# Sharing two of a quad's 32 score tiles between ScalarE and VectorE in the second full-attention layer

## The chip, the core and the metric

The kernel runs on one core of a Trainium2 chip. Its engines are TensorE (PE, with its weight loads as PEld), VectorE (DVE), ScalarE (ACT), GpSimd (POOL) and SyncE (SP), which here issues the DMAs. The metric is the device time of one execution in microseconds (us); lower is better. A difference under 0.2% is not told from no change.

## The reference

Four attention layers follow each other on x of 2048 positions by 512 features; layers 0 and 2 use weights A and a window of 256 keys, layers 1 and 3 use weights B and all keys. Everything is float32, with 32 heads of 16 features.

```python
def _B_ref(x, wqkv, wo):                     # _A_ref: the same, with a causal window of 256
    B, S, D = x.shape                        # 1, 2048, 512
    H = 32; Dh = D // H
    qkv = (x @ wqkv).reshape(B, S, 3, H, Dh).transpose(2, 0, 3, 1, 4)
    q, k, v = qkv[0], qkv[1], qkv[2]
    scores = jnp.einsum("bhqd,bhkd->bhqk", q, k) * Dh ** -0.5
    p = softmax(scores, axis=-1)
    o = jnp.einsum("bhqk,bhkd->bhqd", p, v)
    return o.transpose(0, 2, 1, 3).reshape(B, S, D) @ wo

x = A_x
x = x + _A_ref(_layernorm(x), A_wqkv, A_wo)
x = x + _B_ref(_layernorm(x), B_wqkv, B_wo)
x = x + _A_ref(_layernorm(x), A_wqkv, A_wo)
x = x + _B_ref(_layernorm(x), B_wqkv, B_wo)
```

## The kernel before, in words

The layers are numbered 0 to 3 (`l`); layer 3 is the second full one. In a full layer the work is cut into quads: `c` is one of 4 blocks of 512 queries, `qd` one of 8 groups of 4 heads. Layer 3 goes through them as `t` (two groups of heads) outside, `c` next and the two `qd` inside, 32 quads in all.

Within a quad, `attn_full` runs over 16 tiles `j` of 128 keys, and in each over two pairs of heads `pr`. `exps` writes the transposed scores of one tile and one pair, 128 keys by 2 heads by 512 queries, into a score buffer `s` of two PSUM banks, one bank for each head (L764, eight matmuls of 32 keys each). There are two such buffers. ScalarE then takes both banks in one instruction, exp(scale x s), into a tile `e` of SBUF (L772). There is no maximum to subtract here: a bound on the scores is added inside the matmul by extra rows of the keys and queries. The matmuls with the values follow about two tiles later, when `flush` runs the closure `pv` (L817): eight for a tile, four heads by two halves of the keys, each head into its own 32 partitions of the accumulators `acc`. A column of ones in the values `V` gives the softmax's denominator, and `epilogue` divides at the end of a quad, so a factor common to all of a quad's exponentials drops out.

Between the tiles stands side work: projections of queries, keys and values for later quads and the output projection of earlier ones. `Side.step` and `Side.share` deal it out in small pieces by a modelled clock, a budget and a `lag` that holds pieces back while PE is charged with more than its share. Its results collect in one PSUM buffer `b`, and VectorE joins the two halves into SBUF (L428, L429 by `join`, or L714 for the output). VectorE's short operations wait in queues `VQ`, which `drain` hands out one at a time by the same clock, the queue with the lowest number first.

In layer 3 the orders of PE and of VectorE are those in which the code is written out; the other engines' orders are made by a scheduler. The tag `xh` has four buffers of 2 KB per partition; the layer norms of earlier layers used them.

Of the kernel before, what the change touches and what calls it, by code (L numbers as in the profile page):

```python
# [9 lines left out]
F32 = mybir.dt.float32  # L10
# [3 lines left out]
I32 = mybir.dt.int32  # L14
AF = mybir.ActivationFunctionType
ALU = mybir.AluOpType
# [3 lines left out]
P = 128  # L20
NT = S // P
# [3 lines left out]
QC = 512  # L25
# [165 lines left out]
def fast_path(ctx, tc, flag, a_x, a_wqkv, a_wo, b_wqkv, b_wo, out):  # L191
# [20 lines left out]
    XC, XN, V, O, OT, KM, PH = {}, {}, {}, {}, {}, {}, {"free": 0.0, "busy": False}  # L212
# [13 lines left out]
    def vec(us):  # L226

        vt_[0] = max(vt_[0], clock[0]) + us
# [59 lines left out]
    nc.gpsimd.memset(onesf, 1.0)  # L288
    nc.gpsimd.memset(ones, 1.0)
    nc.gpsimd.memset(zeros, 0.0)  # L290

    nc.gpsimd.memset(hsum, 1.0)
    nc.gpsimd.affine_select(hsum, hsum, pattern=[[-DH, 32]], compare_op=ALU.is_ge,
# [458 lines left out]
        if u:  # L752
            soon(1, 1.2, parts)

    def exps(name, kt, qt, pr, pieces):

        ps = ps_s.tile([P, 2, QC], F32, name=f"s{name}", tag="s")
        w0 = min(p[3] for p in pieces)
        w1 = max(p[3] + p[2] for p in pieces)
        for kc, qc, wd_, s0 in pieces:  # L760
            if PH["full"]:
                for g in range(0, P, 32):
                    for h in range(2):
                        nc.tensor.matmul(ps[g:g + 32, h], kt[R * h:R * h + R, pr, kc + g:kc + g + 32],  # L764
                                         qt[R * h:R * h + R, pr], start=True, stop=True, skip_group_check=True)
                continue
            for h in range(2):
                nc.tensor.matmul(ps[:, h, s0:s0 + wd_], kt[R * h:R * h + R, pr, kc:kc + P],  # L768
                                 qt[R * h:R * h + R, pr, qc:qc + wd_], start=True, stop=True)
        spent(0.27)  # L770
        e = pp.tile([P, 2, QC], F32, name=f"e{name}", tag="e", bufs=EB)
        nc.scalar.activation(e[:, :, w0:w1], ps[:, :, w0:w1], AF.Exp, scale=SCALE)  # L772
        return e

    def flush(n):
# [27 lines left out]
        return kt, qt  # L803

    def attn_full(l, c, qd, kt, qt, a):
        for j in range(NT):
            es_ = []
            for pr in range(2):
                es_.append(exps(f"{l}_{c}_{qd}_{j}_{pr}", kt[j // 8], qt, pr, [(j % 8 * P, 0, QC, 0)]))
                if pr == 0:  # L810
                    yield None

            def pv(j=j, es_=es_):
                for h in range(4):
                    for r in range(2):
                        k = slice(R * r, R * r + R)
                        nc.tensor.matmul(acc[r][32 * h:32 * h + DH + 1, :], V[l, qd // 4, j // 8][k, j % 8, 4 * (qd % 4) + h, :],  # L817
                                         es_[h // 2][k, h % 2, :], start=(j == 0), stop=(j == NT - 1),
                                         skip_group_check=True)
            yield pv  # L820


# [202 lines left out]
    def attention(l, works):  # L1025

        win = l % 2 == 0
        phase(l)
        load = load_win if win else load_full
        sd = None  # L1030
        for t in range(NHT if l == 3 else 1):
            for c in range(NQ):
                qds = range(2 * t, 2 * t + 2) if l == 3 else range(NQD)
                if l == 1:

                    sd = sd or Side(NT * NQD // 2, works[0], works[1], 0.33)
                    while ("Q", 1, c) not in DONE or pend and PH["busy"]:
                        sd.one(True)
                    settle()
                else:  # L1040
                    sd = Side((3 if win else NT) * len(qds), works[t * NQ + c], works[t * NQ + c + 1], 0.34 if l == 3 and t < 2 else 0.0)
                ahead = deque([PRE.pop("w", None) or load(l, c, qds[0])])
                if win:
                    ahead.append(load(l, c, 1))
                for qd in qds:
                    if (l, c, qd) == (1, 0, NQD // 2):
                        sd.finish()
                        sd = Side(NT * NQD * NQ - NT * NQD // 2, works[1], works[2], 0.33)
                    while (l, c, qd % 2) == (1, 0, 1) and qd + 1 in qds and ("S", 1, (qd + 1) // 2) not in DONE:
                        if ("K1", (qd + 1) // 2) in DONE and not PH["busy"]:  # L1050
                            settle()
                        else:
                            sd.one(True)
                    ops = ahead.popleft()
                    if qd + 1 + win in qds:
                        ahead.append(load(l, c, qd + 1 + win))
                    a = acc[qd % 2 if win else 0]
                    began, u = clock[0], 0
                    for f in (attn_win if win else attn_full)(l, c, qd, *ops, a):
                        drain()  # L1060
                        if f is None:
                            flush(1)
                            if u == 1:
                                sd.step()
                            continue
                        clock[0] = max(clock[0], began + (2.4 if win else 1.8))
                        began = clock[0]
                        pvq.append([f])
                        if win:
                            flush(2)  # L1070
                            sd.step()
                            settle(False)
                        elif u == 0:
                            flush(1)
                        elif u:
                            sd.step()
                        while not win and (c, qd, u) == (0, 0, NT - 5) and ("V", l, 3, (0,), 2) not in DONE:
                            sd.one(True)
                        drain()
                        u += 1  # L1080
                    pvq[-1].append(lambda l=l, c=c, qd=qd, a=a: epilogue(l, c, qd, a))
                if l != 1 or c == NQ - 1:
                    sd.finish(l == 3 and (t, c) != (NHT - 1, NQ - 1))
                if not win and not PH["busy"]:
                    settle()
        flush(0)
        drain(4)
        phase(None)
# [208 lines left out]
```

## Time and profile before

| | us |
|---|---|
| median of 3 runs | 2695.24 (2694.04 to 2697.39) |
| profiled execution | 2692.26 |
| its span, from the first to the last instruction | 2690.2 |
| first exponential of layer 3 starts | 1709.2 |
| last exponential of layer 3 starts | 2669.2 |

The prediction quotes rows of the profile. In a row of a group, the line and engine come first, then the operation, what it writes and reads, partitions by elements, and the count; after the bar the busy time in us and the mean length of one in ns; after the second bar the engine's idle time just before these instructions and which instructions ended it. In a timeline row the first two numbers are start and length in us, and instructions of one kind are merged. Successive instructions of one engine overlap a little, so lengths add up to more than the time that they take together. The TensorE clock granted is 0.991 of full speed over the span.

### The profile page before, as it was taken

How to read it: one execution, taken by the hardware profiler on the slowest of the kernel's cores; microseconds unless marked ns; L12 is line 12 of the kernel's file. 1: busy time of each engine (PE TensorE's matmuls, PEld its weight loads, DVE VectorE, ACT ScalarE, POOL GpSimd, SP SyncE). 2: the span in 40 equal slices, each digit the busy share in tenths (PEclk: the TensorE clock that was granted, in tenths of full speed). 3: DMA queues.
4: the chain of work that ended last, by engine and by line, in shares of the span. 5: the costliest groups of instructions: out<-in, count | busy, mean ns of one | idle time of the engine just before them, and what ended most of it. 6: DMA issues, size and time to landing. Idle time of an engine off the chain costs nothing.

```text
span 2690.2 us, 120844 instructions
## 1 busy us (share of the span) xinstructions
PE 2474.9 (92%) x54767; PEld 1133.5 (42%) x54767; DVE 1107.5 (41%) x2350; ACT 2363.6 (88%) x2671; POOL 531.8 (20%) x1072
## 2 busy tenths in 40 slices
PE   7889999999998999999999999899999999999997
PEld 3344444444443444444444444544444443433332
DVE  5576453223334434434236666232333323333333
ACT  4666764999999999999996776699999999999997
POOL 1556550000000100100116886010000000000000
PEclk9999999999999999999999999999999999999999
DMA  8889875232334325324227666433333323334332
GB/s 281 254 274 268 236 198 155 69 97 86 110 94 120 97 91 148 103 87 115 92 77 211 189 171 166 128 95 105 98 97 97 106 77 114 106 98 126 126 118 93
DMA packets 341189, 361.29 MB, mean 134 GB/s; under 512 B 117800, under 2 KB 256568, under 8 KB 334392
## 3 DMA queue, kind: packets, MB, share of 16 engines
q1 hardware_dynamic: 340664, 353.46, 44.2%
q8 instruction: 430, 7.05, 1.1%
q14 instruction: 95, 0.78, 0.1%
HBM read 240.65 MB, written 96.99 MB: 126 GB/s over the span
## 4 chain that ended last, share of the span: by engine, by line
ACT 55%; PE 23%; issue 11%; DVE 6%; DMA 3%; SPq 1%; POOL 0%; ACTq 0%; DVEq 0%; POOLq 0%
ACT e L772 55%; PE b L406 7%; PE acc L850 4%; PE acc L817 3%; PE s L764 2%; PE s L768 2%; PE bs L409 2%; PE b L409 2%; PE b L402 1%; DMA kt<-kw 1%; DVE xh L461 1%; DVE xn L455 0%; DMA qs<-sp 0%; SPq L483 0%; DVE xh L455 0%
## 5 line engine op out<-in xcount | busy, mean ns | idle before, releaser
L772 ACT ACTIVATE e<-s 128x1024 f32<-128x1024 f32 (+2 forms) x2432 | 2241.6, 1056 | 143.2 <-PE s L768 104.5
L817 PE MATMUL acc<-e,vt 64*17 64x512 f32 x16384 | 1094.6, 590 | 1.9 <-issue 1.9
L764 PE MATMUL s<-qt,kt 64*32 64x512 f16 x16384 | 860.0, 381 | 123.9 <-ACT e L772 97.1
L764 PEld LDWEIGHTS <-kt 64*32 64x32 f16 x16384 | 408.2, 89 | 935.1 <-issue 853.8
L817 PEld LDWEIGHTS acc<-e,vt 64*17 64x17 f32 x16384 | 283.8, 92 | 67.9 <-issue 8.1
L843 POOL TENSOR_SCALAR_AFFINE_SELECT e<-e 128x256 f32<-128x256 f32 x512 | 230.5, 457 | 154.8 <-ACT e L772 154.1
L840 POOL TENSOR_SCALAR_AFFINE_SELECT e<-e 128x256 f32<-128x256 f32 x448 | 201.5, 456 | 96.5 <-ACT e L772 93.2
L850 PE MATMUL acc<-e,vt 128*17 128x384 f32 (+2 forms) x2816 | 202.6, 390 | 2.5 <-POOL e L840 2.2
L749 POOL TENSOR_TENSOR oh<-o,oh 128x512 f16<-128x512 f32 x31 | 36.1, 1165 | 725.1 <-DVE oh L748 725.1
L428 DVE TENSOR_SCALAR sa<-acc 128x512 f32<-128x512 f32 x64 | 44.3, 691 | 291.3 <-PE acc L817 291.3
L406 PE MATMUL b<-xc,w 128*32 128x512 f16 x2496 | 152.4, 389 | 10.8 <-DVE km L575 6.9
L714 DVE SCALAR_TENSOR_TENSOR x<-b,x 128x512 f32<-128x512 f32 x122 | 84.0, 689 | 175.1 <-PE b L402 168.4
L534 POOL TENSOR_TENSOR sq_h<-sp_h 128x512 bf16<-128x512 f16 x29 | 43.0, 1483 | 562.4 <-DVE sp_h L528 562.4
L768 PE MATMUL s<-qt,kt 64*128 64x384 f16 (+2 forms) x1408 | 120.8, 276 | 28.2 <-ACT e L772 22.7
L534 POOL TENSOR_TENSOR sq<-sp 128x512 bf16<-128x512 f16 x32 | 45.8, 1434 | 496.8 <-DVE sp L528 473.6
L402 PE MATMUL b<-xc,w 64*32 64x512 f16 x3072 | 126.4, 376 | 1.5 <-DVE j L429 0.8
L428 DVE TENSOR_SCALAR vt<-b 128x256 f32<-128x256 f32 (+1 forms) x36 | 18.4, 512 | 233.8 <-PE b L402 219.9
L402 PE MATMUL b<-wo,oh 64*32 64x512 f16 x2592 | 109.1, 376 | 4.1 <-DVE m_None L591 1.8
L402 PE MATMUL b<-xc,w_h 64*32 64x512 f16 x2784 | 111.8, 376 | 0.1
L428 DVE TENSOR_SCALAR j_h<-b 128x512 f32<-128x512 f32 x29 | 20.1, 692 | 214.6 <-PE b L402 214.6
L406 PEld LDWEIGHTS <-w 128*32 128x32 f16 x2496 | 73.5, 99 | 79.2 <-issue 27.7
L768 PEld LDWEIGHTS <-kt 64*128 64x128 f16 x1408 | 52.2, 94 | 125.7 <-issue 105.3
(142 smaller groups left out, 1942.3 us busy)
## 6 DMA issues: line engine op xcount, KB each, us to landing
kt<-kf SPq DMA_DIRECT2D x128, 512.0 KB
qt<-qs SPq DMA_DIRECT2D x128, 256.0 KB
xd<-x SPq DMA_DIRECT2D x96, 256.0 KB
x<-xd SPq DMA_DIRECT2D x96, 256.0 KB
w<-wd SPq DMA_DIRECT2D x21, 1024.0 KB
kt<-kw SPq DMA_DIRECT2D x64, 256.0 KB
qs<-sp SPq DMA_DIRECT2D x48, 256.0 KB
wo<-wd SPq DMA_DIRECT2D x12, 1024.0 KB
```

The costliest lines, as they stand in the source:

```text
L402: nc.tensor.matmul(ps[g:g + 32, r], a[k, g:g + 32], b[k], start=(i == 0), stop=(i == len(pairs) - 1), skip_group_check=True)
L406: nc.tensor.matmul(ps[g:g + 32], a[:, g:g + 32], b, start=(i == 0), stop=(i == len(pairs) - 1), skip_group_check=True)
L409: nc.tensor.matmul(ps, a, b, start=(i == 0), stop=(i == len(pairs) - 1))
L534: nc.gpsimd.tensor_tensor(sq, sp[:, 0], sp[:, 0], ALU.mult)
L714: nc.vector.scalar_tensor_tensor(xs[i], p, 1 / WS, xs[i], op0=ALU.mult, op1=ALU.add)
L764: nc.tensor.matmul(ps[g:g + 32, h], kt[R * h:R * h + R, pr, kc + g:kc + g + 32], qt[R * h:R * h + R, pr], start=True, stop=True, skip_grou ...
L768: nc.tensor.matmul(ps[:, h, s0:s0 + wd_], kt[R * h:R * h + R, pr, kc:kc + P], qt[R * h:R * h + R, pr, qc:qc + wd_], start=True, stop=True)
L772: nc.scalar.activation(e[:, :, w0:w1], ps[:, :, w0:w1], AF.Exp, scale=SCALE)
L817: nc.tensor.matmul(acc[r][32 * h:32 * h + DH + 1, :], V[l, qd // 4, j // 8][k, j % 8, 4 * (qd % 4) + h, :], es_[h // 2][k, h % 2, :], star ...
L840: nc.gpsimd.affine_select(v, v, pattern=[[0, 2], [-1, P]], compare_op=ALU.is_gt, fill=0.0, base=0, channel_multiplier=1)
L843: nc.gpsimd.affine_select(v, v, pattern=[[0, 2], [1, P]], compare_op=ALU.is_ge, fill=0.0, base=0, channel_multiplier=-1)
L850: nc.tensor.matmul(a[32 * h:32 * h + DH + 1, q * P:(q + nb) * P], V[l, (4 * c + j) // 4][:, j % 4, 4 * qd + h, :], es_[h // 2][:, h % 2, s ...
```

## The change: VectorE makes one head of two tiles

In layer 3, the second pair of heads (`pr` = 1) of key tiles `j` = 4 and `j` = 9 is shared. ScalarE takes one bank of 512 columns; VectorE reads the other (`OWN` says which) and makes its exponential in eight instructions. The first scales the score to a base-2 exponent in fixed point, bounds it from below and writes it as int32. Two bit operations split that into a power of two `e` and a fraction `u`, and five steps of a polynomial give `p`. The first is issued at once; the other seven go into a new queue `VQ[4]`, behind the four that there were. The tiles `u`, `e` and `p` use the tag `xh`. The polynomial's form gives twice the exponential, so each of ScalarE's exponentials of this layer gets the bias ln 2, from a tile of 128 by 1 that POOL fills at the start. The matmuls of `pv` leave the two heads out, and `late` issues them together behind tile 14 of the quad; it first hands out what is left of `VQ[4]`.

```diff
+OWN = {4: 1, 9: 0}
+POLY = (-0.2122642642036666, 20.582234973412888, 57.43304580516819, 188.4105936388931, 265.3878017523131)
+OWN_AT = 12
+LEAD, LOW = 0x40000000 | 0x761904, -117.0
...
-    VQ, vt_ = [deque() for _ in range(4)], [0.0]
+    VQ, vt_ = [deque() for _ in range(5)], [0.0]
...
+    ln2 = cp.tile([P, 1], F32, name="ln2")
+    nc.gpsimd.memset(ln2, 0.6931471805599453)
...
+    def own_exp(name, s, got):
+
+        u, e, p = (vp.tile([P, QC], F32, name=f"{n}{name}", tag="xh", bufs=XNB) for n in ("ou", "oe_", "op_"))
+        ui, ei = u.bitcast(I32), e.bitcast(I32)
+        with tc.high_priority(HEAD_START):
+            nc.vector.tensor_scalar(ui, s, SCALE * 1.4426950408889634 * 2.0 ** 23, LOW * 2.0 ** 23, op0=ALU.mult, op1=ALU.max)
+        vec(0.75)
+        ops = [(0.45, lambda: nc.vector.tensor_scalar(ei, ui, 0x7F800000, LEAD, op0=ALU.bitwise_and, op1=ALU.bitwise_xor)),
+               (0.45, lambda: nc.vector.tensor_scalar(ui, ui, 0x7FFFFF, 0x3E800000, op0=ALU.bitwise_and, op1=ALU.bitwise_or))]
+        for i, k in enumerate(POLY):
+            ops.append((0.7, lambda i=i, k=k: nc.vector.scalar_tensor_tensor(p, p if i else u, k / 4.0 ** (i + 1), e if i == 4 else u,
+                                                                            op0=ALU.add, op1=ALU.mult)))
+        got["left"] = got.get("left", 0) + len(ops)
...
+        for us, f in ops:
+            VQ[4].append((clock[0] + 0.6, us, lambda f=f: one(f)))
+        return p
...
-        nc.scalar.activation(e[:, :, w0:w1], ps[:, :, w0:w1], AF.Exp, scale=SCALE)
+        if own is not None:
+            nc.scalar.activation(e[:, 1 - own], ps[:, 1 - own], AF.Exp, bias=ln2, scale=SCALE)
+            got[name] = own_exp(name, ps[:, own], got)
+        elif got is not None:
+            nc.scalar.activation(e, ps, AF.Exp, bias=ln2, scale=SCALE)
+        else:
+            nc.scalar.activation(e[:, :, w0:w1], ps[:, :, w0:w1], AF.Exp, scale=SCALE)
...
+                own = OWN.get(j) if l == 3 and pr else None
+                es_.append(exps(f"{l}_{c}_{qd}_{j}_{pr}", kt[j // 8], qt, pr, [(j % 8 * P, 0, QC, 0)], own, got))
...
+                mine = OWN if l == 3 else {}
+                for h in range(4):
+                    if j not in mine or h != 2 + mine[j]:
+                        head(j, h, es_[h // 2][:, h % 2], j == NT - 1)
+
+                def late():
+                    while got["left"]:
+                        vec(VQ[4][0][1])
+                        VQ[4].popleft()[2]()
+                    for i, own in mine.items():
+                        head(i, 2 + own, got[f"{l}_{c}_{qd}_{i}_1"], False)
+                    spent(0.86)
+                if j == OWN_AT and mine:
+                    PH["late"] = late
...
                         elif u:
+                            if PH["late"]:
+                                PH["late"]()
+                                PH["late"] = None
+                                sd.lag += 0.86
                             sd.step()
```

The rows below show the program's order of instructions on an engine. Names are those of the code with block, quad, tile and pair: `e_2_3_4_1` belongs to block 2, quad 3, tile 4, pair 1 (all rows are of layer 3). ScalarE around that tile, before:

```order
L772 ACTIVATE e_2_3_3_1_46688<-s_2_3_3_1_46679 128x1024
L772 ACTIVATE e_2_3_4_0_46699<-s_2_3_4_0_46690 128x1024
L772 ACTIVATE e_2_3_4_1_46718<-s_2_3_4_1_46709 128x1024
L772 ACTIVATE e_2_3_5_0_46768<-s_2_3_5_0_46759 128x1024
```

and after:

```order
L803 ACTIVATE e_2_3_3_1_46949<-s_2_3_3_1_46940,ln_88 128x1024
L803 ACTIVATE e_2_3_4_0_46960<-s_2_3_4_0_46951,ln_88 128x1024
L800 ACTIVATE e_2_3_4_1_46979<-s_2_3_4_1_46970,ln_88 128x512
L803 ACTIVATE e_2_3_5_0_47025<-s_2_3_5_0_47016,ln_88 128x1024
```

The tile of pair 1 is half as long, and every row reads the bias tile besides its scores.

VectorE around the same tile, before (`j` and `vt` are joins of a query projection and of a value projection, `m` and `km` belong to the bound on the scores):

```order
L428 TENSOR_SCALAR j_1_2_h_2_46657<-b_37140 128x512
L429 SCALAR_TENSOR_TENSOR j_1_2_h_2_46657<-b_37140,j_1_2_h_2_46657 128x512
L528 CAST sp_1_2_h_2_46720<-j_1_2_h_2_46657 128x512
L529 TENSOR_TENSOR sp_1_2_h_2_46720<-j_1_2_h_2_46657,sp_1_2_h_2_46720 128x512
L428 TENSOR_SCALAR vt_1_1_43761<-b_37140 128x16x16
L429 SCALAR_TENSOR_TENSOR vt_1_1_43761<-b_37140,vt_1_1_43761 128x16x16
```

and after, with the read of the score bank at L766:

```order
L434 TENSOR_SCALAR j_1_2_h_2_46918<-b_37142 128x512
L435 SCALAR_TENSOR_TENSOR j_1_2_h_2_46918<-b_37142,j_1_2_h_2_46918 128x512
L766 TENSOR_SCALAR ou_2_3_4_1_46981<-s_2_3_4_1_46970 128x512
L534 CAST sp_1_2_h_2_47009<-j_1_2_h_2_46918 128x512
L535 TENSOR_TENSOR sp_1_2_h_2_47009<-j_1_2_h_2_46918,sp_1_2_h_2_47009 128x512
L768 TENSOR_SCALAR oe_2_3_4_1_46982<-ou_2_3_4_1_46981 128x512
L769 TENSOR_SCALAR ou_2_3_4_1_46981<-ou_2_3_4_1_46981 128x512
L771 SCALAR_TENSOR_TENSOR op_2_3_4_1_46983<-ou_2_3_4_1_46981 128x512
L771 SCALAR_TENSOR_TENSOR op_2_3_4_1_46983<-op_2_3_4_1_46983,ou_2_3_4_1_46981 128x512 x2
L434 TENSOR_SCALAR vt_1_1_43958<-b_37142 128x16x16
L435 SCALAR_TENSOR_TENSOR vt_1_1_43958<-b_37142,vt_1_1_43958 128x16x16
L771 SCALAR_TENSOR_TENSOR op_2_3_4_1_46983<-op_2_3_4_1_46983,ou_2_3_4_1_46981 128x512
```

The read stands behind a join here, and the polynomial's steps stand between the joins that the side work needs.

PE at the end of the same quad, before, goes from the last scores of tile 14 to the first of tile 15:

```order
L764 LDWEIGHTS kt_2_3_1_45812
L764 MATMUL s_2_3_14_1_47221<-qt_2_3_45808,kt_2_3_1_45812 32x512
L764 LDWEIGHTS kt_2_3_1_45812
L764 MATMUL s_2_3_15_0_47232<-qt_2_3_45808,kt_2_3_1_45812 32x512
L764 LDWEIGHTS kt_2_3_1_45812
```

and after:

```order
L791 LDWEIGHTS kt_2_3_1_46051
L791 MATMUL s_2_3_14_1_47490<-qt_2_3_46047,kt_2_3_1_46051 32x512
L853 MATMUL acc_81<-op_2_3_4_1_46983,vt_0_0_36722 17x512
L853 MATMUL acc_82<-op_2_3_4_1_46983,vt_0_0_36722 17x512
L853 MATMUL acc_81<-op_2_3_9_1_47246,vt_0_1_36956 17x512
L853 MATMUL acc_82<-op_2_3_9_1_47246,vt_0_1_36956 17x512
L562 LDWEIGHTS hsum
L562 MATMUL b_37142<-sq_0_3_h_1_46619,hsum 32x512
```

Four matmuls on VectorE's `op` tiles now stand there, and behind them, in this quad, a piece of side work (L562) that stood elsewhere.

More of the change, by code (lines that the diff above doesn't have):

```diff
@@ L210, in fast_path @@
             for ty in range(2) for s in range(4)}
-    XC, XN, V, O, OT, KM, PH = {}, {}, {}, {}, {}, {}, {"free": 0.0, "busy": False}
+    XC, XN, V, O, OT, KM, PH = {}, {}, {}, {}, {}, {}, {"free": 0.0, "busy": False, "late": None}
     WT, ST, pend = {}, {}, []
-    VQ, vt_ = [deque() for _ in range(4)], [0.0]
+    VQ, vt_ = [deque() for _ in range(5)], [0.0]
     clock, DONE, XNR, ONR = [0.0], {}, {}, {}
@@ L753, in epilogue, with one, exps @@
             soon(1, 1.2, parts)
-    def exps(name, kt, qt, pr, pieces):
+    def own_exp(name, s, got):
[10 more added lines that the diff above has]
+        got["left"] = got.get("left", 0) + len(ops)
+        def one(f):
+            f()
+            got["left"] -= 1
+        for us, f in ops:
+            VQ[4].append((clock[0] + 0.6, us, lambda f=f: one(f)))
+        return p
+    def exps(name, kt, qt, pr, pieces, own=None, got=None):
         ps = ps_s.tile([P, 2, QC], F32, name=f"s{name}", tag="s")
@@ L805, in attn_full @@
     def attn_full(l, c, qd, kt, qt, a):
+        got = {} if l == 3 else None
         for j in range(NT):
@@ L813, in pv, with head @@
             def pv(j=j, es_=es_):
-                for h in range(4):
+                def head(j, h, e, last_):
                     for r in range(2):
@@ L817, in pv @@
                         nc.tensor.matmul(acc[r][32 * h:32 * h + DH + 1, :], V[l, qd // 4, j // 8][k, j % 8, 4 * (qd % 4) + h, :],
-                                         es_[h // 2][k, h % 2, :], start=(j == 0), stop=(j == NT - 1),
-                                         skip_group_check=True)
+                                         e[k], start=(j == 0), stop=last_, skip_group_check=True)
+                mine = OWN if l == 3 else {}
[11 more added lines that the diff above has]
+                    PH["late"] = late
             yield pv
```

1 line of the change is left out of this document (removed).

## The prediction

> **What bounds the kernel now.** I read the page's first part, then the busy times of the second full layer alone, then the chain of waits and the groups of instructions there, and last the order in time of single instructions.
>
> ```profile
> PE 2474.9 (92%) x54767; PEld 1133.5 (42%) x54767; DVE 1107.5 (41%) x2350; ACT 2363.6 (88%) x2671; POOL 531.8 (20%) x1072
> ```
>
> Over the whole span TensorE (PE) looks busier than ScalarE (ACT), but the change touches only the last of four layers. Its exponentials run from 1709.2 to 2670.3 us. The busy times of that stretch (sum row left out), and the shares of the chain of waits in 1800 to 2600 us:
>
> ```profile
> 1709.00:2671.00 962.00, 877.19 (x21814) 388.75 (x21806) 310.03 (x582) 944.75 (x1024) 57.51 (x42) 1.00 0.35 104
> ```
> ```profile
> by line: ACT e L772 76.8%; issue 14.6%; PE acc L817 3.0%; PE s L764 2.3%; PE b L402 0.9%; DVE m L590 0.5%; DVE m L591 0.5%; PE b L556 0.4%; DMA qt<-qs 0.4%; DVE x L714 0.3%; DVE sa L429 0.2%; DMA qs<-m 0.2%; ACTq L772 0.0%; DVE ot L731 0.0%
> ```
>
> The columns of the first row are PE, PE's weight load, DVE (VectorE), ACT and POOL; the clock is 1.00. ACT works 944.75 of 962 us, PE 877 of 962, and the chain goes through the exponential (L772). The groups of this stretch say what each of the two waits for:
>
> ```profile
> L772 ACT ACTIVATE e<-s 128x1024 f32<-128x1024 f32 x1024 | 944.7, 1072 | 18.0 <-PE s L764 17.5
> L817 PE MATMUL acc<-e,vt 64*17 64x512 f32 x8192 | 546.5, 590 | 1.9 <-issue 1.9
> L764 PE MATMUL s<-qt,kt 64*32 64x512 f16 x8192 | 427.7, 381 | 74.9 <-ACT e L772 59.0 <-DMA kt<-mk 1.8 <-DMA qt<-qs 0.9
> ```
>
> ACT is idle for 18.0 us in all and PE waits for ACT for 59.0 us. So ScalarE bounds this layer almost everywhere: what one of its 1024 exponentials costs more or less goes 1:1 into the time. The pace comes from the last row of the timeline of ACT and the range of one record:
>
> ```profile
> 2241.91 117.96 ACT L772 ACTIVATE e<-s 128x1024 f32<-128x1024 f32 x128 [1.21 <-PE s L764]
> 2361.08 309.16 ACT L772 ACTIVATE e<-s 128x1024 f32<-128x1024 f32 x336 [1.21 <-PE s L764]
> L772 ACT ACTIVATE e<-s x1024: 1017/1085/1092, 1709.2 to 2669.2; 128x1024 f32<-128x1024 f32 x171
> ```
>
> 336 exponentials without a gap take 309.16 us. One record is 1.085 us long, but the next starts before it ends: (309.16 - 1.085) / 335 = 0.9196 us is the true pace.
>
> **The change part by part.** *Shorter exponentials.* Of 32 quads (4 blocks of queries by 8 groups of heads) each has 2 shared tiles, so 64 of 1024 exponentials go from 1024 to 512 columns. A 512-column exponential is in the trace of the window layers:
>
> ```profile
> 109.47 1.09 ACT L772 ACTIVATE e<-s 128x512 f32<-128x512 f32 x2 [0.88 <-PE s L768]
> L772 ACT ACTIVATE e<-s 128x512 f32<-128x512 f32 x32 | 18.0, 598 | 5.3 <-PE s L768 5.2
> ```
>
> Two back to back take 1.09 us, one record 0.598, so the pace is 0.49 us. Each shared tile saves 0.92 - 0.49 = 0.43 us of ACT, 64 x 0.43 = **-27.5 us**.
>
> *A bias from a tile.* The diff gives every exponential of this layer, all 1024 and not only the 64, `bias=ln2`, where ln2 is a 128x1 tile in memory; before, bias and scale were constants of the instruction. No exponential of the trace has such an operand. The nearest rows are the layer norm's activation L458, which takes bias and scale both from tiles, and the weight split L325, which takes neither; both read 128x512 f32 from SBUF and write f16, four back to back:
>
> ```profile
> 1688.47 2.93 ACT L458 ACTIVATE xh<-x,nb,y 128x512 f16<-128x512 f32 x4 [1.25 <-DVE nb L450]
> 104.53 2.19 ACT L325 ACTIVATE w<-wr 128x512 f16<-128x512 f32 x4
> L458 ACT ACTIVATE xh<-x,nb,y x8: 797/799/813, 427.2 to 1690.6; 128x512 f16<-128x512 f32 x8
> L325 ACT ACTIVATE w<-wr x32: 612/626/649, 11.9 to 196.9; 128x512 f16<-128x512 f32 x32
> ```
>
> L458's pace is (2.93 - 0.80) / 3 = 0.710 us, L325's (2.19 - 0.626) / 3 = 0.521 us. Two tile operands cost 0.189 us of pace, not of latency alone, since these are back to back. For one operand the ends are 0 (all of it is the scale's, or it hides where the data come from PSUM) and 0.189 (all of it is the bias's); I take half, 0.0945 us, as both are operands of one kind and one shape. 1024 x 0.0945 = **+96.8 us**. This is the largest term, and it is dearer than the saving. By the difference of the records' lengths, (797 - 626) / 2 = 0.0855 us, it would be +87.6 us.
>
> The Trainium skill (ScalarE: Activation LUTs, section What ACT_TABLE_LOAD costs) states what the trace can't split: about 93 ns for each pointer operand. By it the term would be 1024 x 0.093 = 95 us, an estimate from that page; its 186 ns for two agrees with the measured 189, but no run here shows one alone, nor one with data from PSUM.
>
> *VectorE's share.* Rows of DVE in this layer:
>
> ```profile
> L428 DVE TENSOR_SCALAR j_h<-b 128x512 f32<-128x512 f32 x27 | 18.7, 692 | 205.0 <-PE b L402 205.0
> L529 DVE TENSOR_TENSOR sp_h<-j_h,sp_h 128x512 f16<-128x512 f32 x27 | 18.7, 692 | 0.9
> L528 DVE CAST sp_h<-j_h 128x512 f16<-128x512 f32 x27 | 11.5, 427 | 1.9 <-DVE j_h L429 0.4
> ```
>
> The read of the bank is like L428 from PSUM, 0.69 us. The two bit operations read one SBUF tile: 0.43 us each by L528, 0.69 at most by the other two rows. The five polynomial steps read two operands: 0.69 each by L529. That is 0.69 + 0.86 + 3.46 = 5.0 us a tile, 64 x 5.0 = 321 us. DVE's work in the layer grows from 310 to some 631 us of a layer that then lasts over 1000: no new bound, off the path except at two hand-overs.
>
> First hand-over: PE may refill a score buffer only when both readers are done, and there are two buffers. The timeline of PE and ACT shows the room:
>
> ```profile
> 2454.03 5.67 ACT L772 ACTIVATE e<-s 128x1024 f32<-128x1024 f32 x6
> 2454.47 1.05 PE L817 MATMUL acc<-e,vt 64*17 64x512 f32 x16
> 2456.08 0.41 PE L764 MATMUL s<-qt,kt 64*32 64x512 f16 x8
> 2456.23 0.69 DVE L428 TENSOR_SCALAR j_h<-b 128x512 f32<-128x512 f32 x1 [11.63 <-PE b L402]
> 2456.96 0.69 DVE L429 SCALAR_TENSOR_TENSOR j_h<-b,j_h 128x512 f32<-128x512 f32 x1
> ```
>
> Exponentials start at 2454.03 + n x 0.92, so 2456.79; the tile written at 2456.08 is ready at 2456.49, 0.3 us ahead. A free DVE would be done 0.7 us after that, ACT's half (0.49 + 0.09 us) 0.9 us after it: no cost. If DVE is in the join of a projection (the last two rows, 1.4 us), it is late by up to 1.4 us, of which the following full exponential (1.01 us, less the 0.41 us to write the scores) covers 0.6 and the 0.2 us above some more. Ends: 0, and 64 x 0.5 = 32 us; queued behind the read are DVE's later joins, for which PE's single projection buffer waits. DVE is busy about a third of the time before this work, so I take 0.1 us a tile, **+6 us**.
>
> Second hand-over: the two postponed heads' matmuls stand behind tile 14, in PE's order, and wait for DVE's last step. Five tiles (9 us) lie between the second read and them, against 4.3 us of steps. They use two of four column groups for what a whole step of four heads needs, while the steps for tiles 4 and 9 still run the other heads and get no shorter: at most 1.05 us (the L817 row above) more PE work a quad, 34 us in all. PE has 85 us to spare in the layer and more when ACT slows; side work yields, since the diff charges 0.86 to its lag. Ends 0 and 0.6 us a quad (19 us); I take 0.1, near the idle PE, **+3 us**.
>
> *Stalls that go.* Of ACT's 18.0 us of idle time a part is PE being late after bursts of side work. The two blocks of 96 projection matmuls at the end of a group of quads disappear from PE's order, and a slower ACT gives PE 0.09 us more for each tile. Ends 0 and -18; I take **-5 us**, since only two tiles of head start exist. The SP queue's loads and stores of the layer swap places by a few rows and none is added, with key and query loads done well ahead (DMA waits 2.7 us in the L764 row): nothing. The 128x1 fill on POOL stands at the start: nothing.
>
> Sum: 96.8 - 27.5 + 6 + 3 - 5 = +73.3 us. The profiled execution took 2692.26 us (span 2690.2 and 2.1 around it), which gives 2765.6; the median of the runs, 2695.24, lies 3.0 above it, so **2768 us**, 2.7% slower. Without the bias operand the same sum would be a gain of 23 us.
>
> **Rivals.** *The bias is free (other side).* The read of a 128x1 operand could hide behind the PSUM stream of the exponential before, or L458's whole extra could be the scale's. Against it: L458's extra shows in the pace as well as in the record, and nothing distinguishes the two operands. For it: all rows with operands from tiles read SBUF data. The time is 2695.2 - 27.5 + 9 - 5 = 2672 us. It decides once the operand costs under (27.5 - 4) / 1024 = 0.023 us.
>
> *VectorE gives banks back late.* If DVE's queue makes most shared tiles stall ACT by 0.5 us (32 us) and the postponed matmuls wait in each quad (19 us), the time is 2768 + 26 + 16 = 2810 us. For it: reads stand right behind a join in some quads. Against: DVE is free two thirds of the time.
>
> *The bias carries all of the 0.189 us:* 2768 + 97 = 2865 us; unlikely, by symmetry.
>
> *It comes out even:* a price near 0.02 us, which no row suggests.
>
> **How the numbers follow.** My forecast 0.76, free bias 0.13, late banks 0.06, dear bias 0.02, even 0.03. A difference of 0.2% (5 us) is about what this kernel's runs can tell. Faster 0.13, within it 0.03, slower 0.84. Range: the forecast's low end has the price by record length (-9), all 18 us of stalls gone (-13) and no new ones (-9), and comes to 2737; its high end, with half of the hand-overs' bounds, is 2768 + 26 = 2794. So 2738 to 2796 for 8 in 10; the free bias and most of the late banks lie outside.
>
> **What would show it.** In the profile after: the full exponentials' pace near 1.014 us where they run without gaps (a record some 0.09 longer than 1.085), the half ones' near 0.585; quads of 31.6 us instead of 29.4; DVE near 630 us in the layer; PE waiting for ACT longer than 59 us; ACT's idle time below some 25 us, mostly put down to the scores. A pace still at 0.92 refutes the main term. Idle time of ACT above 50 us, released by PE behind a DVE read or by the postponed matmuls, would make the two hand-overs mine to have undersized.

## The result, and the profile after

The changed kernel takes 2833.14 us (median of 4 runs, 2828.09 to 2838.51) against 2694.64 us for the kernel before on the same chip: a ratio of 1.0514 (95% interval 1.0488 to 1.0540), 5.1% slower. The direction was forecast; the size was not, 2768 us with a range to 2796. The profiled execution took 2838.51 us with a span of 2836.5.

The first part of the page, and the busy times of the second full layer (PE, PE's weight load, DVE, ACT, POOL, then clock, DMA share and GB/s):

```profile
PE 2541.8 (90%) x54767; PEld 1128.1 (40%) x54767; DVE 1443.8 (51%) x2862; ACT 2443.1 (86%) x2671; POOL 529.3 (19%) x1073
1709.00:2850.00 1141.00, 954.11 (x21880) 390.24 (x21878) 656.57 (x1120) 1026.77 (x1030) 57.74 (x42) 0.98 0.30 90
```

In this row ACT is busy 1026.8 us instead of 944.8, and DVE 656.6 instead of 310.0 (648.6 up to 2819 us, where the layer's exponentials are over). PE is busy 954.1 us instead of 877.2 with nearly the same number of matmuls; why was not followed, but the clock granted to it was 0.98 in this stretch and 1.00 before. And ACT is no longer busy all the time. The groups of this layer by shape, with idle time behind the second bar:

```profile
L803 ACT ACTIVATE e<-s,ln 128x1024 f32<-128x1024 f32 x958 | 985.0, 1131 | 77.7 <-PE s L791 76.1
L791 PE MATMUL s<-qt,kt 64*32 64x512 f16 x8184 | 454.2, 385 | 142.2 <-ACT e L803 91.4 <-DMA qt<-qs 32.1 <-DMA kt<-mk 1.8
L771 DVE SCALAR_TENSOR_TENSOR op<-op,ou 128x512 f32<-128x512 f32 x192 | 141.9, 739 | 5.4
```

ACT's idle time went from 18.0 to 77.7 us, and PE has a releaser that was 0.9 us before and is 32.1 us now: the load of the queries (`qt<-qs`). The order in time of ACT's work in one quad shows the rest:

```profile
1979.52 20.30 ACT L803 ACTIVATE e<-s,ln 128x1024 f32<-128x1024 f32 x20 [0.19 <-PE s L791]
1999.65 0.76 ACT L800 ACTIVATE e<-s,ln 128x512 f32<-128x512 f32 x1
2000.41 1.11 ACT L803 ACTIVATE e<-s,ln 128x1024 f32<-128x1024 f32 x1
2001.72 8.14 ACT L803 ACTIVATE e<-s,ln 128x1024 f32<-128x1024 f32 x8 [0.19 <-PE s L791]
2009.70 0.74 ACT L800 ACTIVATE e<-s,ln 128x512 f32<-128x512 f32 x1
...
2021.20 11.23 ACT L803 ACTIVATE e<-s,ln 128x1024 f32<-128x1024 f32 x11 [0.30 <-PE s L791]
```

Twenty full exponentials without a gap take 20.30 us, so the pace is (20.30 - 1.12) / 19 = 1.009 us, where it was 0.920. From a shared tile's exponential (L800) at 1999.65 to the start of the second one behind it at 2001.72 pass 2.07 us, as much as two full ones take (2.02): a gap of 0.19 us stands one tile behind each shared one. A gap of 0.30 us or more stands once in most quads. The 32 quads take 1098.8 / 32 = 34.3 us each (below), where 31.6 were forecast without gaps; before it was 960.0 / 32 = 30.0.

The layer can be added up. From the start of its first exponential to the start of its last it took 960.0 us before and 1098.8 us now (1718.5 to 2817.3), 138.8 us more. Of that, 960 full exponentials at 0.090 us more are 86, and ACT's additional idle time is 77.7 - 18.0 = 60. The remainder, 138.8 - 86 - 60, is -7 us: what 64 half exponentials save by themselves, before the gaps that they cause. It is a rough figure, since a pace of 1.004 us in place of 1.009 would make it -2. (In the profiled run the layer starts 9 us later than before, 1718.5 against 1709.2 us. The layers ahead of it are not changed, and in the profiles of the runs below the layer starts anywhere from 1706.5 to 1714.8.)

### The profile page after: what moved, and what is told of

The parts are those of the page before. It is cut to its first block, busy times and chain, and to the rows that moved or that the text cites. A ratio compares the mean times of both kernels' runs of the same rounds, so it can differ in the third digit from the quotient of the medians.

```text
span 2836.5 us, 121356 instructions
## 1 busy us (share of the span) xinstructions
PE 2541.8 (90%) x54767; PEld 1128.1 (40%) x54767; DVE 1443.8 (51%) x2862; ACT 2443.1 (86%) x2671; POOL 529.3 (19%) x1073
## 4 chain that ended last, share of the span: by engine, by line
ACT 46%; PE 30%; issue 14%; DVE 5%; DMA 4%; SPq 1%; POOL 0%; ACTq 0%; DVEq 0%; POOLq 0%
ACT e L805 26%; ACT e L803 20%; PE b L412 8%; PE acc L853 6%; PE s L791 5%; PE acc L899 4%; PE s L795 2%; PE bs L415 2%; PE b L415 1%; PE b L408 1%; DMA kt<-kw 1%; DMA qt<-qs 1%; DMA x<-in_A_x_dram 1%; DVE xh L467 1%; DMA qs<-m 1%
## 5 line engine op out<-in xcount | busy, mean ns | idle before, releaser
L805 ACT ACTIVATE e<-s 128x1024 f32<-128x1024 f32 (+2 forms) x1408 | 1297.1, 1045 | 134.1 <-PE s L795 112.5
L853 PE MATMUL acc<-e,vt 64*17 64x512 f32 x16128 | 1115.4, 595 | 0.3 <-issue 0.3
L791 PE MATMUL s<-qt,kt 64*32 64x512 f16 x16384 | 887.7, 383 | 194.1 <-ACT e L803 91.4
L803 ACT ACTIVATE e<-s,ln 128x1024 f32<-128x1024 f32 x960 | 987.0, 1131 | 77.7 <-PE s L791 76.1
L853 PEld LDWEIGHTS acc<-e,vt 64*17 64x17 f32 x16128 | 294.2, 93 | 71.9 <-issue 9.9
L771 DVE SCALAR_TENSOR_TENSOR op<-op,ou 128x512 f32<-128x512 f32 x192 | 141.9, 739 | 5.4
L766 DVE TENSOR_SCALAR ou<-s 128x512 int32<-128x512 f32 x64 | 44.3, 692 | 192.3 <-ACT e L800 192.3
L434 DVE TENSOR_SCALAR j<-b 128x512 f32<-128x512 f32 x32 | 22.0, 689 | 203.8 <-PE b L408 203.8
L408 PE MATMUL b<-wo,oh 64*32 64x512 f16 x2592 | 119.9, 379 | 4.7 <-DVE m_None L597 1.8
L408 PE MATMUL b<-xc,w_h 64*32 64x512 f16 x2784 | 123.1, 376 | 0.0
```

What stands on the lines that cost most here:

```text
L408: nc.tensor.matmul(ps[g:g + 32, r], a[k, g:g + 32], b[k], start=(i == 0), stop=(i == len(pairs) - 1), skip_group_check=True)
L771: ops.append((0.7, lambda i=i, k=k: nc.vector.scalar_tensor_tensor(p, p if i else u, k / 4.0 ** (i + 1), e if i == 4 else u, op0=ALU.add, ...
L803: nc.scalar.activation(e, ps, AF.Exp, bias=ln2, scale=SCALE)
```

## The experiments

The theory after the result had four parts: the bias operand costs about 92 us; the load of the next queries is late and costs some 33 to 48; the shared tiles save nothing since their two readers go one after the other; the postponed matmuls leave a gap in each quad. The rivals were that VectorE's load as such holds up the joins, and that one large cause carries the others. The ratios below are against the kernel before on the chip of that run, where its median was 2692.66 to 2694.60 us; a difference in us between two versions is that of their medians, and can be off by some 2 us where the chips differ.

**The bias alone.** The kernel before, with the bias tile on the layer's 1024 exponentials and nothing else:

```diff
+    ln2 = cp.tile([P, 1], F32, name="ln2")
+    nc.gpsimd.memset(ln2, 0.6931471805599453)
...
-        nc.scalar.activation(e[:, :, w0:w1], ps[:, :, w0:w1], AF.Exp, scale=SCALE)
+        if name[0] == "3":
+            nc.scalar.activation(e, ps, AF.Exp, bias=ln2, scale=SCALE)
+        else:
+            nc.scalar.activation(e[:, :, w0:w1], ps[:, :, w0:w1], AF.Exp, scale=SCALE)
```

> The kernel before, with one edit: all 1024 exponentials of layer 3 take their bias from the 128x1 tile (the common factor 2 drops out in the softmax). Theory 1 (the operand costs 0.09 us of ScalarE's pace, whatever else the change does): pace 1.01 us without gaps, 2694.6 + 1024 x 0.090 = 2787 us, less a few us of stalls that go: 2775 to 2790. Rival (part of the pace seen after the change comes from VectorE's or TensorE's new work in the memories): pace near 0.95, under 2740 us.

Measured: 2776.77 us, ratio 1.0307 (1.0284 to 1.0329), +82 us. The group and the last row of ACT's timeline:

```profile
L775 ACT ACTIVATE e<-s,ln 128x1024 f32<-128x1024 f32 x1024 | 1030.7, 1294 | 11.4 <-PE s L766 11.3
2416.51 337.67 ACT L775 ACTIVATE e<-s,ln 128x1024 f32<-128x1024 f32 x336 [0.95 <-PE s L766]
```

The pace is (337.67 - 1.3) / 335 = 1.004 us against 0.9196 of the same row before: 0.0845 us each, 86.5 us in all. ACT's idle time falls from 18.0 to 11.4 us, since PE has longer for each tile. 86.5 - 6.6 = 80, and the run gave 82. That one operand is 59% of the whole loss, and it hits every exponential, though only 64 tiles needed their factor made equal.

**A constant bias.** The changed kernel with the same ln 2 as a constant of the instruction:

```diff
-            nc.scalar.activation(e, ps, AF.Exp, bias=ln2, scale=SCALE)
+            nc.scalar.activation(e, ps, AF.Exp, bias=0.6931471805599453, scale=SCALE)
```

(and the same for the half ones)

> The changed kernel with ln 2 as a constant of the instruction instead of the tile, nothing else. Theory 1 (bias, hand-over of shared tiles and late query loads add up): 2833 - 92 + some 5 to 15 us of stalls that a faster ScalarE uncovers, 2745 to 2756 us, so still slower than before, with full exponentials back at 0.92 us. Rival (the hand-overs alone bound the layer, and the operand hides behind them): above 2790 us.

Measured: 2771.74 us, ratio 1.0289 (1.0268 to 1.0309). Taking the tile away brought 61 us, neither the 77 to 88 that the first theory wanted nor the under 43 of the rival. The rows say why it is less than the price of the operand:

```profile
L803 ACT ACTIVATE e<-s 128x1024 f32<-128x1024 f32 x960 | 905.4, 1048 | 107.3 <-PE s L791 98.7
1932.79 10.35 ACT L803 ACTIVATE e<-s 128x1024 f32<-128x1024 f32 x11 [1.15 <-PE s L791]
```

The exponentials are fast again, (10.35 - 1.05) / 10 = 0.93 us, but ACT is idle for 107.3 us instead of 77.7, and the gap behind the postponed matmuls, 0.30 us in most quads before this edit, is now 1.0 to 1.15 us in five of the nine quads from 1720 to 2000 us. The slow exponential had hidden part of PE's lateness.

**The query loads.** Below are PE's scores at the start of a new block of queries in the changed kernel, with the work that they wait for (SPq is the queue of DMA issues):

```profile
2265.44 0.69 DVE L596 TENSOR_SCALAR m<-b 32x512 f16<-32x512 f32 x1 [1.96 <-DMA kf<-mk]
2266.16 0.69 DVE L597 SCALAR_TENSOR_TENSOR m<-b,m 32x512 f16<-32x512 f32 x1
2266.88 0.28 SPq L609 DMA_DIRECT2D qs<-m  x1
2268.94 0.87 SPq L820 DMA_DIRECT2D qt<-qs  x2
2274.78 0.63 PE L791 MATMUL s<-qt,kt 64*32 64x512 f16 x8 [10.13 <-DMA qt<-qs]
2275.53 1.11 ACT L803 ACTIVATE e<-s,ln 128x1024 f32<-128x1024 f32 x1 [9.65 <-PE s L791]
2276.87 0.67 PE L791 MATMUL s<-qt,kt 64*32 64x512 f16 x8
2277.67 1.11 ACT L803 ACTIVATE e<-s,ln 128x1024 f32<-128x1024 f32 x1 [1.02 <-PE s L791]
```

The row `m` of the bound on the scores is joined at 2266.85, written to memory, read back with the queries, and PE stands still until 2274.78 and ACT until 2275.53. The last two rows show that such a wait costs more than its own length. The clock granted to TensorE fell to 0.50 here while PE stood still, and was still 0.50 up to 2278 us. At that clock the eight matmuls of a tile's scores take 0.63 and 0.67 us instead of 0.41, and ACT has a second gap of 1.02 us. The same is seen at six of the seven waits, and ACT's gaps behind them add up to some 9 us. Counted by ACT's exponentials, `m`, and with it the squares from which it comes, stands at tiles 14 and 15 of the quad ahead in these seven cases; before the change it stood at tiles 6 to 8 in five of them, and at 12 and 13 in two. They are placed by `settle`, which `share` calls only once the modelled clock has passed VectorE's modelled time; the new queue `VQ[4]` keeps VectorE's time ahead until the quad's end. The edit lets that one rule tolerate 0.9 us more while the new queue holds something:

```diff
-            if pend and not PH["busy"] and clock[0] >= max(PH["free"], pend[0][0], vt_[0] - 0.2):
+            if pend and not PH["busy"] and clock[0] >= max(PH["free"], pend[0][0], vt_[0] - 0.2 - (0.9 if VQ[4] else 0.0)):
```

> The changed kernel; the rule that settles a finished projection's squares (it waits until VectorE's modelled time is no more than 0.2 us ahead) tolerates 0.9 us more while polynomial steps are queued, so that the squares of the next block's queries stand at tiles 4 to 10 instead of 14 and 15 of a quad. The lag charge stays. Theory 1 (these squares are late because the new queue keeps VectorE's modelled time ahead): the waits of the scores for the query load (32 us) go, and with them most of the 5 to 10 us gaps of ScalarE at block ends: 2785 to 2800 us. Rival (the lag charge, or VectorE's real backlog, makes the query projection late): unchanged, 2825 to 2840.

Measured: 2783.46 us, ratio 1.0331 (1.0311 to 1.0351), 50 us less than the changed kernel. For the blocks that waited, `m` now stands at tiles 5 to 12. In the waits of this run the query load has no entry of its own any more, and ACT's group reads:

```profile
L803 ACT ACTIVATE e<-s,ln 128x1024 f32<-128x1024 f32 x960 | 985.3, 1132 | 29.1 <-PE s L791 27.4
```

Idle time falls from 77.7 to 29.1 us, 48.6, which is the whole gain: 32 are the waits for the queries, some 9 the gaps at the low clock behind them, and the rest is not split. The clock granted in the layer is 1.00 again, and VectorE does the same work (1441.0 us busy in the whole run against 1443.8). So the cause is not VectorE's load, but where the planner put the squares.

**A second guess at the same place.** The charge of 0.86 to `lag` behind the postponed matmuls also holds back side work. A rival had it that this charge makes the loads late:

```diff
-                                sd.lag += 0.86
```

> The changed kernel without the charge of 0.86 to the side work's lag in the postponed step. In the program's order the squares of the next block's queries stay at tiles 14 and 15 in most blocks. Theory 1 (VectorE's modelled time, not the lag, keeps them late): the waits for the query load stay, 2825 to 2842 us. Rival (the lag charge made the query projection late): 2785 to 2800.

Measured: 2850.94 us, ratio 1.0584 (1.0567 to 1.0602), slower than with it. The rival is refuted. Theory 1 had expected 2825 to 2842 and was missed too: without the charge the queries' loads are waited for longer.

```profile
PE s L791 <- DMA qt<-qs: 43.3, 7, 12.7
```

(total us, times, longest; the changed kernel had 32.1, 7, 10.1.) How the additional side work delays them further was not followed.

**Two readers of one tile.** The first tile of the timeline below is a shared one in the changed kernel. ACT's half stands first, then PE's refill of the other buffer, then DVE's read:

```profile
1901.58 0.69 ACT L800 ACTIVATE e<-s,ln 128x512 f32<-128x512 f32 x1
1901.74 0.41 PE L791 MATMUL s<-qt,kt 64*32 64x512 f16 x8 [0.16 <-ACT e L803]
...
1902.27 1.12 ACT L803 ACTIVATE e<-s,ln 128x1024 f32<-128x1024 f32 x1
1902.30 0.69 DVE L766 TENSOR_SCALAR ou<-s 128x512 int32<-128x512 f32 x1 [3.19 <-ACT e L800]
...
1903.04 0.41 PE L791 MATMUL s<-qt,kt 64*32 64x512 f16 x8
...
1903.58 5.13 ACT L803 ACTIVATE e<-s,ln 128x1024 f32<-128x1024 f32 x5 [0.19 <-PE s L791]
```

VectorE has been idle for 3.19 us and reads another bank, yet it starts 0.03 us after ACT's half ends. The program has a semaphore wait on ScalarE in front of that read, because both read one tile. The waits of the whole layer say that this is so each time:

```profile
DVE ou L766 <- ACT e L800: 192.3, 64, 13.4
```

So the buffer comes back at 1902.99 and not at 1902.27; PE refills it at 1903.04, and ACT, through with the next full exponential at 1903.39, has to wait until 1903.58. The experiment gives the two heads of a shared tile a PSUM tile of one bank each, in the place of the second buffer (the pool is exchanged ahead of a shared tile and behind it):

```diff
-        ps = ps_s.tile([P, 2, QC], F32, name=f"s{name}", tag="s")
+        ps = scores(f"s{name}", pr, own is not None)
+        row = (lambda h: ps[h]) if own is not None else (lambda h: ps[:, h])
...
-            nc.scalar.activation(e[:, 1 - own], ps[:, 1 - own], AF.Exp, bias=ln2, scale=SCALE)
-            got[name] = own_exp(name, ps[:, own], got)
+            nc.scalar.activation(e[:, 1 - own], row(1 - own), AF.Exp, bias=ln2, scale=SCALE)
+            got[name] = own_exp(name, row(own), got)
```

> The changed kernel with the scores of the 64 shared tiles in two one-bank tiles instead of one of two banks, so that the program no longer makes VectorE's read wait for ScalarE's half (before this edit it waits for it 64 times). Theory 1 (this wait passes on to TensorE, which refills the buffer late, and costs the 0.19 us gap and more behind each shared tile): the gaps go; but a half exponential can't end sooner than TensorE refills the other buffer, some 0.7 us, so 0.2 to 0.3 us for each of 64 tiles: 2813 to 2822 us. Rival (VectorE is late by its own queue, not by the wait): unchanged, above 2827.

Measured: 2815.75 us, ratio 1.0445 (1.0425 to 1.0465), 17 us less. The same place now:

```profile
1991.00 0.69 DVE L786 TENSOR_SCALAR ou<-s_1h 128x512 int32<-128x512 f32 x1 [2.85 <-PE s_1h L812]
1991.13 0.76 ACT L821 ACTIVATE e<-s_1h,ln 128x512 f32<-128x512 f32 x1
...
1991.36 0.41 PE L812 MATMUL s<-qt,kt 64*32 64x512 f16 x8 [0.31 <-ACT e L824]
...
1991.83 8.27 ACT L824 ACTIVATE e<-s,ln 128x1024 f32<-128x1024 f32 x8
```

Both readers run at once, VectorE even first, and the gap of 0.19 us is gone. The rows show a second limit: the half exponential starts at 1991.13 and the next one at 1991.83, 0.70 us later, although two half ones in a row had a pace of 0.49 us in the window layers. The next scores are written into the other buffer from 1991.36 to 1991.77, so they were not there sooner: PE waits for the full exponential ahead (`<-ACT e L824`), which reads that buffer.

**The postponed matmuls.** First the changed kernel without them, so that their part of the sums over keys is missing:

```diff
-                    for i, own in mine.items():
-                        head(i, 2 + own, got[f"{l}_{c}_{qd}_{i}_1"], False)
```

> The changed kernel with the postponed matmuls of the two heads left out (their part of the sum over keys is missing); bias tile, one score tile and late squares as they are. Theory 1 (the postponed step stalls ScalarE also where an exponential takes 1.01 us, but less, since TensorE has more room: 0.30 us is the gap seen behind most of them): 10 to 15 us less, 2818 to 2823 us. Rival (as dear as with the constant bias, 31 us): 2802.

Measured: 2819.56 us, ratio 1.0461 (1.0441 to 1.0480), 13.6 us less than the changed kernel, 0.42 us a quad where 0.1 was forecast. In the profiled runs the layer, from its first exponential to its last, is 11.9 us shorter (1086.9 against 1098.8).

**The repairs together.** Constant bias and query loads, both edits above:

> Constant bias and the early squares together; shared tile and postponed matmuls as in the changed kernel. Theory 1 (late query loads are a cost of their own, 40 us of waits in the run with constant bias): 2771.7 - 45 = 2727 us, 2720 to 2738. Rival (the waits only move to other places once ScalarE is fast): above 2750.

Measured: 2721.96 us, ratio 1.0114 (1.0097 to 1.0132). The two add up: 61 + 50 = 111 us off 2833.1. With the tile of one bank for each head as well:

> Constant bias, early squares and two one-bank tiles. Theory 1: a shared tile and its follower take 0.76 + 1.02 + 0.19 = 1.97 us with the one tile and constant bias, more than the 1.84 of two full ones; with two tiles 0.70 + 0.92 = 1.62: 64 x 0.35 = 22 us less than the run with constant bias and early squares, about 2705 us (2698 to 2712). What is then left above the kernel before, some 10 us, is 64 x 0.22 = 14 us of gain against some 1 us a quad that ScalarE stands still behind the postponed matmuls. Rival (half exponentials reach their 0.49 us): under 2690.

Measured: 2710.23 us, ratio 1.0070 (1.0054 to 1.0085): 12 us, not the 22 expected. And with the postponed matmuls left out of that, as above:

> The same as the run with constant bias, early squares and two one-bank tiles, with the postponed matmuls of the two heads left out (their part of the sum over keys is missing; the charge to the modelled clock and lag stays, so the order of all else is the same). Theory 1 (the postponed step costs about 1 us of ScalarE's time in each of 32 quads): 25 to 35 us less, 2670 to 2682 us, which is the kernel before less 14 to 25 us. Rival (TensorE has the room, the postponed step is free): within 5 us of the run with them.

Measured: 2679.42 us, ratio 0.9954 (0.9940 to 0.9967). The quads of ACT around 2250 to 2285 us, first with the postponed matmuls, then without:

```profile
2249.71 9.48 ACT L824 ACTIVATE e<-s 128x1024 f32<-128x1024 f32 x10
2259.91 10.34 ACT L824 ACTIVATE e<-s 128x1024 f32<-128x1024 f32 x11 [0.72 <-PE s L812]
```
```profile
2263.50 0.63 ACT L821 ACTIVATE e<-s_1h 128x512 f32<-128x512 f32 x1
2264.17 19.65 ACT L824 ACTIVATE e<-s 128x1024 f32<-128x1024 f32 x21
```

Without them ACT goes 21 exponentials without a gap; with them it stops once in the quad. Leaving them out brings 31 us, about 1 us for each of the 32 quads: with fast exponentials the two score buffers don't cover the time that PE spends on them. What is left, 15 us under the kernel before, is what the sharing itself gives here when the two heads' matmuls are free: 15 / 64 = 0.23 us a tile, which agrees with the start-to-start times of a half exponential (2263.50 to 2264.17, 0.67 us) against 0.92 of a full one.

**Making room for them.** The last attempt keeps the postponed matmuls, one tile later, and issues no side work in that step:

```diff
-OWN_AT = 12
+OWN_AT = 13
...
-                            sd.step()
+                                sd.k += 1
+                            else:
+                                sd.step()
```

> The same as the run with constant bias, early squares and two one-bank tiles, with the postponed matmuls one tile later and no side work dealt out in that step. Theory 1 (the stall behind them is TensorE with more work in a step than the two score buffers cover, 0.44 us of scores, twice 0.85 of values and up to 0.33 of side work against 1.84): the stall falls from about 1 us to some 0.3 a quad, 2680 to 2692 us, which would be faster than the kernel before by 0.1 to 0.5%. Rival (the stall is TensorE waiting for VectorE's last polynomial step): no further than 5 us, since that step is also later.

Measured: 2729.44 us, ratio 1.0137 (1.0119 to 1.0155): missed by 37 us on the wrong side. ACT waits for the scores a third less, 25.9 us instead of 37.2, and the layer from first to last exponential is 972.4 us long instead of 979.2; but PE's timeline behind the layer's last exponential has this:

```profile
2689.63 0.84 PE L428 MATMUL b<-wo,oh 64*32 64x512 f16 x24 [1.52 <-DVE x L740]
...
2707.10 1.48 PE L428 MATMUL b<-wo,oh 64*32 64x512 f16 x24 [1.53 <-DVE x L740]
```

About 20 us of output projection was not placed in the layer and runs alone at the end, each piece waiting for VectorE to empty the one buffer. So a step taken from the side work was paid at the end. No version that does the whole computation came out under the kernel before; the best is 0.7% above it.

## Why the prediction was right or wrong, point by point

| term | forecast, us | shown, us |
|---|---|---|
| bias from a tile | +96.8 | +82 alone; 86 in the changed kernel's pace |
| shorter exponentials | -27.5 | -7 without the gaps that follow; -15 at best |
| first hand-over | +6 | +17 |
| second hand-over | +3 | +14 (31 with fast exponentials) |
| SP queue and loads | 0 | +50 (waits 32, low clock behind them 9, rest not split) |
| stalls that go | -5 | -7 with the bias alone, hidden under new ones after |

*Bias operand: right.* Half of the 0.189 us of the two-operand row was the right choice, and that it counts in the pace and for all 1024 was the right reading; it measured 0.085 to 0.090 us. The Trainium skill (ScalarE: Activation LUTs, section What ACT_TABLE_LOAD costs) states about 93 ns for each pointer operand, and these runs, with data from PSUM, agree within 9 ns. The sign named for it, a record 0.09 us longer, did not show (the median went from 1.085 to 1.124 us); the pace is what carries the cost. The rivals of a free bias and of all 0.189 us are both refuted by the bias alone.

*Shorter exponentials: the step that failed is "64 x 0.43".* It took 0.49 us from half exponentials back to back. In the layer no half one follows another: a full one stands on either side, and only two score buffers exist. The next scores can be begun when the full exponential before has ended and take 0.41 us to write. With the wait ahead of them and the start behind them that is some 0.70 us, and it stays at 0.67 to 0.71 with the faster constant bias. So the forecast pace of 0.585 never appeared, and the sharing could give 0.22 to 0.25 us a tile and not 0.43. The row with the 0.41 us for the scores was quoted in the prediction, for another purpose.

*First hand-over: the failed assumption is that both readers start when the scores are there.* The prediction asked how late a busy VectorE could be, and found room. VectorE was idle; the order came from the program, which makes one reader of a tile wait for the other. The time lost, 0.19 us of gap and some 0.1 us of overlap that an exponential ahead of a gap doesn't have, for each of 64, measured 17 us, inside its ends of 0 and 32 but not near the 6 taken. That VectorE would be held up by a join, as the prediction had it, is not what the 64 waits show: they end with L800.

*Second hand-over: undersized.* Its cost was put at 0.1 us a quad, near PE's idle share of the layer; it is 0.42, within the ends of 0 and 0.6. PE's idle time in the layer is made of short waits for a buffer (91.4 us in 232 of them, 0.4 us each); that it could not be saved up for one burst of 1 us is the likely reason, and is not tested by itself. It grows to 1 us a quad when the exponential is fast, as the constant bias showed.

*Loads: the largest miss.* The step "The SP queue's loads and stores of the layer swap places by a few rows and none is added", with loads done well ahead and a cost of nothing, took the waits of before, 0.9 us, for a property of the kernel. They belonged to its old order: the diff adds a queue to VectorE's model, and the rule that places the squares reads that model. The prediction looked at the order of the SP queue, where rows swap places, and not at how far the squares had moved in PE's order, though the last rows shown of PE's order after the change are of that kind (L562, now behind tile 14). Nor had the prediction a term for the granted clock, which was down to 0.50 at six of the seven waits. Its own condition, ACT idle above 50 us released by PE, was met, but named only the two hand-overs as the cause; 49 of the 60 us more belong to neither.

*VectorE no new bound: right.* It was busy 648.6 us to the layer's end against 631 forecast. The polynomial's steps took 0.72 to 0.74 us on average and not 0.69, the two bit operations 0.53 and 0.54 and not 0.43 (their medians are 0.69 and 0.43), and with the query loads repaired the same load of VectorE cost nothing that shows. The rival of late banks had the right kind of mechanism with the wrong owner, and its 2810 was too low as well.

*The parts by experiment.* 82 (bias) + 50 (loads) + 17 (readers) + 14 (postponed) = 163, and the change cost 138.5; the 24 us between them are the saving itself, 64 x (1.01 - 0.70) = 20 us at the slower pace, and 4 that this doesn't split. The four are not strictly additive: taking the bias tile out of the changed kernel brings 61 and not 82. Taken one after the other, the repairs give 61 (constant bias) + 50 (loads) + 12 (separate tiles) + 31 (postponed matmuls left out) = 154 us, from 2833.1 down to 2679.4, which is the loss of 138.5 and the 15 of the saving. The forecast's sum of +73 held the two terms that the diff shows openly and missed the 50 that come through the planner.

*The range.* Its ends as stated, 2738 and 2796, differ a little from its own sums, 2737 and 2794, and the high end sets half of the hand-overs' bounds on top of the 9 us that the forecast already holds; put in their place it would be some 2785. The shorter estimate for the operand sets the shortest record of L458 (797 ns) against the median of L325 (626); with the median of both it is 88.6 us. None of this bears on the miss: 2833 lies beyond every one of these ends, because the loads had no term.

## What to carry to other kernels

Count an edit by all the instructions that it touches: a factor of 2 that 64 tiles needed put an operand of 0.085 us on 1024 instructions of the engine that bounds the layer, and a constant would have done. Before crediting a shorter instruction, ask what the next one waits for: with two buffers, the refill of the other buffer sets a floor (0.70 us here), and two readers of one tile may go one after the other however free the second engine is. Where a planner deals out work by modelled times, a new queue in the model moves work that the diff doesn't name; look in the order for what a late load stands behind, not only whether the load was early before.

## What the runs showed of the hardware

A bias read from a 128x1 tile lengthens the pace of back-to-back exponentials from PSUM by 0.085 to 0.090 us, while a constant bias that isn't zero costs about 0.01 us at most (0.93 against 0.92). The record's length is no sure guide to that: with the bias alone the mean record is 1.294 us, in the changed kernel 1.131, and the pace is 1.004 and 1.009. VectorE and ScalarE read two banks of PSUM at the same time without either getting longer: on average 0.692 and 0.738 us with the banks in separate tiles (the timeline above shows them overlap), 0.692 and 0.736 one after the other. At six of PE's seven waits for the query load (2.4 to 10.1 us each) the clock granted to TensorE was down to 0.50 for some us after PE had started again, with eight score matmuls at 0.63 to 0.70 us instead of 0.41; with the loads in time the layer's clock was 1.00 and not 0.98.
